# Attention and a gated feed-forward in one kernel: one more staging slot, another order of the opening, two buffers for values and earlier reads of the probabilities

## Chip, cores and metric

The kernel runs on one core of one Trainium2 chip. The metric is device time in microseconds (us) of one execution, lower is better; it stands as the median of three runs. TensorE is PE in the profile (PEld is its weight load), VectorE is DVE, ScalarE is ACT, GpSimd is POOL, SyncE is SP.

## What is computed

Attention with 4 batches, 8 heads, 768 positions and a head size of 64 comes first. A key is kept if it is one of the first 8 (global) or at most 95 positions back (local); every head adds a bias that falls with the distance. Then come 3072 tokens of a feed-forward network with a product as its gate.

```python
scores = scale * np.matmul(q, k.transpose(0, 1, 3, 2))
...
bias = -slopes[:, None, None] * dist[None, :, :]
scores = scores + bias[None, :, :, :]
scores = np.where(keep, scores, -1000000000.0)
scores = scores - np.max(scores, axis=-1, keepdims=True)
a = np.exp(scores)
a = a / (np.sum(a, axis=-1, keepdims=True) + 1e-09)
return np.matmul(a, v).astype(np.float32)
...
a = x @ w1
b = x @ w2
h = a * b @ w3
return (h @ w_out).astype(np.float32)
```

w1 and w2 are 512 x 1024, w3 is 1024 x 1024, w_out is 1024 x 512. The weights reach the kernel as 64-bit words, and the kernel turns them into 32-bit floats itself.

## The kernel before

The tokens are cut into 12 chunks of 256. A step takes two of the four head pairs of a chunk, so there are 24 steps, numbered from 0. Numbers that matter are kept as a high and a low part (names ending in h and l), so that one product is three matmuls. Since h @ w_out follows with nothing between, w3 and w_out are first multiplied together: `fold` (L197) sums eight matmuls for one of eight row blocks f, ACT copies the sum to wh (L199), and `low` (L205, on DVE) writes the low part wl.

**What a step does.** `visit` (L650) issues the scores of step s on PE (L488) and the product of earlier probabilities with their values (L597) in two halves; ahead of the second half stands a small ACT copy into the sums (L662). `rows` takes the row extreme on DVE (L504) and the exponential on ACT (L505); `invert` and `softmax` scale the rows (L509 and L510 on DVE, L521 on ACT, L523 on DVE). In steps 0 to 2 the probabilities are turned by PE (L532, L534) and copied by ACT into the tile early (L536, L538). From step 3 on DVE transposes blocks of 32 (L558), SP writes them to DRAM (L560, tile d), and `back` reads them again in another order (L568, tile ph): four reads, two issued by SP and two by ACT. `take` (L57, L58, L635, L640) moves the results of a visit to xh and xl or xr.

Visit s of the opening, up to visit 3, uses the probabilities of step s - 1; from step 5 on visit s uses those of s - 2. Queries with keys (qr, L466) and values (vr, L473) have one buffer each. vr of step s - 1 is loaded during step s, after the visit.

**The feed-forward.** `run` is a generator, and `slices(k)` runs k of its pieces between the parts of a step. A piece is twelve matmuls of a first product (L220 to L222, into m), or some of the last (L241 to L243). After the first of two products ACT copies it (L228) into ring_a; after the second DVE multiplies the two (L230); gh and gl are the parts of that (L232, or L57 and L58).

**The opening.** `first_steps` runs the words of `ORDER`, which sets the order of DVE, SP and PE by hand (ACT is ordered by the scheduler there). `c` and `C` convert one piece of a weight (`begin`: L151, `merge`: L164, the high part on ACT L169, the low part on DVE L181 or, for `C`, on ACT L172 and a DMA of POOL); `fXY` and `r` are folds, `lX` is L205 of block X, `vX` a visit, `aX` its rows, `sX` its scaling (and the loads behind that), `tXY` a turn, `kX` a take, `pX` or `p` a piece of the feed-forward, `q` the low parts that are due. `ORDER3` does the same for step 3. Each weight lands in a numbered slot `raw[n]`, by the list `plan`; a load is issued when every piece that was in its slot is converted.

**The later steps** are a plain loop; PE, ACT, SP and POOL run in the order in which the code is written, DVE in that of the scheduler. From step 7 on every second step adds one row block of the first weights for the end (`mix`, POOL, L859 and L862, into tiles tq and tl); `round_off` (ACT L867 into th, POOL L869) and `keep` (L873, L874, the stores of th and tl to DRAM, tile tw) follow in the next steps. From step 23 on (about 393 us) the last tokens run as products by Strassen's scheme, which read tw back.

Of the kernel before, what the change touches and what calls it, by code (L numbers as in the profile page):

```python
# [10 lines left out]
F32 = mybir.dt.float32  # L11
F32R = mybir.dt.float32r
BF16 = mybir.dt.bfloat16
I32 = mybir.dt.int32
AF = mybir.ActivationFunctionType
ALU = mybir.AluOpType
PSUM = bass.MemoryType.PSUM

B, H, S, D = 4, 8, 768, 64
DM, DF, DO = 512, 1024, 512  # L20
P = 128
NP = H // 2
NQ = 2
# [3 lines left out]
NCC = DM // P  # L27
NFC = DF // P
# [18 lines left out]
c x c C c C f00 z c C f20 f10 f30 C f31 c C m f21 c c f32 c f11 f01 f13 f12 f23 f22 f33 f03 f34 c c f04 x c v0 f15 f14 f05 f24 f25 f02 f16 f07 f27 f26 a0 f17 f36 f35 f06 C s0 r f37 r r t01 r r l2 r c r r t00 r l1 l0 c c v1 r l3 r c r a1 r c l4 r r s1 r r k1 r r t10 r r t11 r r v2 c r l5 r r r c r a2 r q c l6 r s2 k2 r r p C t20 l7 p t21 c p  # L47
# [28 lines left out]
class FeedForward:  # L76
# [3 lines left out]
    def __init__(self, ctx, tc, w1, w2, w3t, w_out, out):  # L80
        self.nc = tc.nc
# [125 lines left out]
    def run(self, c, xh, xl, row, width, last=False):  # L207
# [4 lines left out]
        for f0 in range(0, NFC, nf):  # L212
# [17 lines left out]
            nc.vector.tensor_tensor(out=a, in0=ps, in1=a, op=ALU.mult)  # L230
# [174 lines left out]
def banded(ctx, tc, ff, xp, ns, nt, nf, oki, ident, qk, vx):  # L405
# [22 lines left out]
    ff.more_room(xp)  # L428
    ff.raw[8] = early.bitcast(I32).rearrange("p i m k c -> p i (m k c)")
# [39 lines left out]
    def load_values(c, hp, tag="vr"):  # L469
        b, cb = divmod(c, NCB)  # L470
        nw = 2 * NQ if cb else 2 * NQ - 1
        vr = ld.tile([P, STEP, 2 * NQ, 2 * D], F32, tag=tag, name=f"vr_{c}_{hp}")
        nc.sync.dma_start(out=vr[:, :, :nw], in_=vx[b, cb, hp // STEP, :, :, :nw])  # L473
        return [vr[:, i] for i in range(STEP)]
# [87 lines left out]
    def back(s):  # L562
        if s not in sent:
            return
        x, d = sent.pop(s)
        for b, m0 in enumerate((1, 0, 3, 2)):
            ms = slice(m0, m0 + 5)
            (nc.sync, nc.scalar)[b // 2].dma_start(out=x[b * BK:(b + 1) * BK].rearrange("r k a u c -> r (k a) (u c)")[:, ms], in_=d[:, :, :, b].rearrange("k a r e -> r (k a) e")[:, ms])  # L568
        phs[s] = x
# [138 lines left out]
    def first_steps():  # L708
# [24 lines left out]
        for i in (0, 1, 0, 1, 0):  # L733
            clear(i)
        plan = ["nt", ("a0", 0, 1), ("o0", 0, 0), ("t0", 0, 1), ("o1", 1, 0), ("t1", 1, 1), ("o2", 2, 0), ("t2", 2, 1), ("o3", 3, 0), ("t3", 3, 1), ("o4", 4, 0), ("t4", 4, 1), ("o5", 0, 0), ("t5", 0, 1), "qr",
                ("o6_7", 1), ("t6_7", 2), ("b0", 3), ("b1", 4), ("b2", 5), ("b3", 2), ("w0", 4), ("w1", 6), ("w2", 5), ("w3", 7), ("w4", 6), ("w5", 4), ("w6", 7), ("w7", 4)]
# [117 lines left out]
    def mix(f):  # L854

        th, tl = tg.tile([P, 4, 2 * P], F32R, name="th"), tg.tile([P, 4, 2 * P], F32, name="tl")
        q = tg.tile([P, 2, NCC * P], F32, name="tq")
        for i in range(2):
            nc.gpsimd.tensor_tensor(out=q[:, i], in0=ff.wq[0][:, f, i].bitcast(F32), in1=ff.wq[1][:, f, i].bitcast(F32), op=ALU.add)  # L859
        (b11, b21), (b12, b22) = ((q[:, i, :2 * P], q[:, i, 2 * P:]) for i in range(2))  # L860
        for o, x, y in ((2, b12, b11), (0, b22, tl[:, 2]), (1, b22, b12), (3, b21, tl[:, 0])):
            nc.gpsimd.tensor_tensor(out=tl[:, o], in0=x, in1=y, op=ALU.subtract)  # L862
        mixed.append((f, th, tl))
# [13 lines left out]
    with tc.manual_schedule(engines={mybir.EngineType.PE}):  # L877
        with tc.manual_schedule(engines={mybir.EngineType.DVE, mybir.EngineType.SP}):
            first_steps()
        with tc.manual_schedule(engines={mybir.EngineType.Activation, mybir.EngineType.SP, mybir.EngineType.Pool}):  # L880
            for s in range(SWAP + 1, n):
# [3 lines left out]
                for i, p in enumerate(pairs(s)):  # L885
                    rs.append(rows(*p, ps[i]))
                    if i == 0 and uu is not None:
                        take(sv, uu)
                loads(s + 1, vals=False)
                loads(s - 1, keys=False)  # L890
                back(s - 1)
                if 0 <= s - MIX < 2 * NFC and (s - MIX) % 2:
                    round_off()
# [4 lines left out]
                if mixed:  # L898
                    keep()
                if 0 <= s - MIX < 2 * NFC and (s - MIX) % 2 == 0:  # L900
                    mix((s - MIX) // 2)
                slices(SLICES[s] - 2)
            back(n - 1)
            vrs[n - 1] = load_values(*pairs(n - 1)[0], tag="qr")
# [214 lines left out]
```

## Time and profile before

| | us |
|---|---|
| runs | 532.54, 532.24, 531.98 |
| median of the three | 532.24 |
| the profiled execution | 533.92 |
| its span, first to last instruction | 532.1 |
| PE busy in it | 519.6 |
| DVE, ACT, POOL busy | 338.6, 256.9, 71.4 |

The profiled execution is 1.68 us above the median of the runs, and 1.82 us of its time lie outside its span. TensorE ran at a mean granted clock of 0.999. PE is busy for 98% of the span, so a time that some other engine takes matters only where PE has to stop for it. Busy PE contains the overlap of matmuls that run one behind the other: what a stop costs is read from the starts of two matmuls.

### The profile page before, as it was taken

The numbers are of one execution on the slowest core, as the hardware profiler recorded it, in microseconds if no ns is written. First come the engines' busy times: TensorE is split into PE (matmuls) and PEld (weight loads), VectorE is DVE, ScalarE is ACT, GpSimd is POOL, SyncE is SP. The second block draws the span as 40 slices with busy tenths as digits, with TensorE's granted clock in tenths as the row PEclk, the third lists the DMA queues.
The fourth block names the chain that finished last, engine by engine and source line by source line (L and its number), as shares of the span: only waits on it lengthen the run. The fifth ranks groups of instructions, "written<-read, shape, count | busy, mean of one in ns | idle before, by whom it ended". The sixth has DMA issues, their size and how long they took to land.

```text
span 532.1 us, 11252 instructions
## 1 busy us (share of the span) xinstructions
PE 519.6 (98%) x4260; PEld 412.8 (78%) x4260; DVE 338.6 (64%) x906; ACT 256.9 (48%) x729; POOL 71.4 (13%) x87
## 2 busy tenths in 40 slices
PE   8899999999899999999999999999999999999996
PEld 3345469989888888888888888788888888888884
DVE  7999997976687576665767646687535433434400
ACT  0344776576566554556665554677424322222220
POOL 0000000000225050243215033422000000000000
PEclk9999999999999999999999999999999999999999
DMA  8997855377779766876857598988724322222031
GB/s 303 407 347 247 306 168 184 120 259 238 224 237 289 256 208 204 264 257 205 274 205 251 161 322 246 275 257 281 218 65 132 111 93 80 79 89 70 1 120 44
DMA packets 50653, 107.70 MB, mean 202 GB/s; under 512 B 4768, under 2 KB 28576, under 8 KB 50592
## 3 DMA queue, kind: packets, MB, share of 16 engines
q1 hardware_dynamic: 43056, 99.50, 54.9%
q10 hardware_dynamic: 7392, 6.88, 5.5%
q0 software_dynamic: 144, 0.52, 0.5%
q8 instruction: 35, 0.57, 0.5%
q14 instruction: 26, 0.21, 0.1%
HBM read 69.67 MB, written 36.70 MB: 200 GB/s over the span
## 4 chain that ended last, share of the span: by engine, by line
PE 78%; DVE 14%; DMA 4%; issue 2%; ACT 1%; SPq 1%; ACTq 0%; DVEq 0%
PE m L220 10%; PE m L221 9%; PE m L222 9%; PE a L948 8%; PE o L241 6%; PE o L242 5%; PE o L243 5%; PE v L597 5%; PE s L488 5%; PE ob L968 4%; PE oa L968 4%; PE b L948 4%; PE c L948 2%; DVE t3s L164 2%; DVE wo L164 2%
## 5 line engine op out<-in xcount | busy, mean ns | idle before, releaser
L220 PE MATMUL m<-xh,wqh 128*128 128x512 f32 (+1 forms) x320 | 113.6, 355 | 1.8 <-DVE ring_a L230 1.2
L221 PE MATMUL m<-xl,wqh 128*128 128x512 f32 (+1 forms) x320 | 111.0, 347 | 0.0
L222 PE MATMUL m<-xh,wql 128*128 128x512 f32 (+1 forms) x320 | 110.9, 347 | 0.0
L505 ACT ACTIVATE pr<-pr,mx 128x232 f32<-128x232 f32 (+1 forms) x192 | 88.2, 462 | 10.3 <-DVE mx L504 10.3
L220 PEld LDWEIGHTS m<-xh,wqh 128*128 128x128 f32 x320 | 60.4, 189 | 11.7 <-DVE ring_a L230 1.6
L222 PEld LDWEIGHTS m<-xh,wql 128*128 128x128 f32 x320 | 60.5, 189 | 7.7
L504 DVE CUSTOM_DVE_ANT_0 pr<-s,biasw 128x232 f32<-128x232 f32 x160 | 54.0, 395 | 19.2 <-PE s L488 19.2
L221 PEld LDWEIGHTS m<-xl,wqh 128*128 128x128 f32 x320 | 60.6, 189 | 7.2
L558 DVE STREAM_TRANSPOSE ph<-pr 128x512 f32<-128x512 f32 x84 | 49.1, 641 | 3.2 <-ACT pr L521 2.1
L241 PE MATMUL o<-wh,gh 128*128 128x512 f32 x128 | 50.8, 397 | 0.0
L242 PE MATMUL o<-wl,gh 128*128 128x512 f32 x128 | 49.9, 390 | 0.0
L243 PE MATMUL o<-wh,gl 128*128 128x512 f32 x128 | 49.9, 389 | 0.0
L57 ACT ACTIVATE gh<-ring_a 128x512 fp32r<-128x512 f32 x29 | 18.3, 630 | 50.8 <-DVE ring_a L230 48.0
L230 DVE TENSOR_TENSOR ring_a<-m,ring_a 128x512 f32<-128x512 f32 x32 | 21.8, 683 | 26.2 <-PE m L222 25.7
L869 POOL TENSOR_TENSOR tl<-tl,th 128x512 f32<-128x512 f32 x16 | 21.8, 1384 | 111.4 <-ACT th L867 111.4
L488 PE MATMUL s<-qr 64*64 64x168 f32 (+2 forms) x768 | 36.6, 299 | 0.0
L505 ACT ACTIVATION_READ_ACCUMULATOR pr<-pr,mx 128x1 f32 x192 | 36.2, 189 | 0.0
L597 PE MATMUL v<-ph,vr 64*64 64x64 f32 (+2 forms) x1208 | 34.1, 243 | 1.4 <-DMA ph<-d 1.4
L521 ACT ACTIVATE pr<-pr,sm 128x232 f32<-128x232 f32 (+1 forms) x84 | 33.3, 466 | 2.5 <-DVE sm L510 2.5
L597 PEld LDWEIGHTS v<-ph,vr 64*64 64x64 f32 (+1 forms) x1208 | 32.1, 133 | 2.9 <-DVE mx L504 1.6
L523 DVE TENSOR_SCALAR pr<-pr,sm 128x232 f32<-128x232 f32 (+1 forms) x84 | 30.1, 400 | 1.3
L197 PE MATMUL w<-wo,ta 128*128 128x512 f32 x64 | 29.2, 601 | 1.6 <-DVE ta L164 1.6
(154 smaller groups left out, 849.8 us busy)
## 6 DMA issues: line engine op xcount, KB each, us to landing
d<-ph SPq DMA_DIRECT2D x42, 512.0 KB, 3.4
qr<-qk SPq DMA_DIRECT2D x16, 624.0 KB, 4.5
vr<-vx SPq DMA_DIRECT2D x17, 512.0 KB, 7.0
t<-tw SPq DMA_DIRECT2D x32, 256.0 KB, 3.2
ph<-d SPq DMA_DIRECT2D x42, 160.0 KB, 7.3
ph<-d ACTq DMA_DIRECT2D x42, 160.0 KB, 6.7
out_dram<-ring_o SPq DMA_DIRECT2D x24, 256.0 KB, 2.8
raw<-w3t SPq DMA_DIRECT2D x11, 512.0 KB, 9.4
```

What stands on the lines that cost most here:

```text
L220: nc.tensor.matmul(ps[:, z], lhsT=mh, rhs=xh[:, i], start=i == 0, stop=False)
L221: nc.tensor.matmul(ps[:, z], lhsT=mh, rhs=xl[:, i], start=False, stop=False)
L222: nc.tensor.matmul(ps[:, z], lhsT=ml, rhs=xh[:, i], start=False, stop=i == NCC - 1)
L241: nc.tensor.matmul(ps, lhsT=gh[:, f, ts], rhs=self.wh[:, f], start=f == 0, stop=False)
L242: nc.tensor.matmul(ps, lhsT=gh[:, f, ts], rhs=self.wl[:, f], start=False, stop=False)
L243: nc.tensor.matmul(ps, lhsT=gl[:, f, ts], rhs=self.wh[:, f], start=False, stop=f == NFC - 1)
L488: nc.tensor.matmul(ps[u][g * HQ:(g + 1) * HQ, j, cols], lhsT=m[:, q0:q0 + HQ], rhs=m[:, j * SLOT:][:, cols], start=True, stop=True)
L504: nc.vector.tensor_tensor_reduce(out=pr[:, j, u, w0:], in0=ps[u][:, j, w0:UW], in1=bias, scale=-SCALE, scalar=3.0e38, op0=ALU.add, op1=ALU ...
L505: nc.scalar.activation(pr[:, j, u, w0:], pr[:, j, u, w0:], AF.Exp, bias=m, scale=-1.0, accum_out=sm[:, j, u:u + 1])
L558: nc.vector.transpose(x[:, k, :, u1 - 4 + u0:u1], units[:, u0:, k0:k0 + P].rearrange("p u (b c) -> p b u c", c=BK))
L597: nc.tensor.matmul(uu[i][u * D:(u + 1) * D, j * P + q:j * P + q + n], lhsT=v[r], rhs=x[:, q // step:(q + n) // step][r], start=k == 0 and ...
L948: nc.tensor.matmul(ps, lhsT=a, rhs=b, start=first and k == 0 and i == 0, stop=k == HC - 1 and i == 2, skip_group_check=True)
```

## The change

The edits, in the order of the diff:

- `ORDER`: l3 moves to right behind l0; l4 to before a1; l6 from behind the conversion of a weight to before `r q c`; s2 behind `k2` and two folds, where it stood ahead of k2; one more piece `p` between l7 and t21.
- The product L230 (L231 after the change) is marked as high priority for the scheduler of DVE.
- A staging slot 9 of 8 KB per partition (two rows of 1024 words): it shares its room with the tiles of `mix`, which now are one tile (tt) in place of th, tl and tq. Weights w4 and w7 go to slot 9 (before: 6 and 4).
- Values have two buffers; in the loop vr of step s, not of s - 1, is loaded in step s. The last values no longer use the room of qr.
- All four reads of the probabilities are issued by SP, and in the loop `back` stands ahead of the loads of qr and vr.
- `round_off` stands behind softmax and `send` of its step, `keep` in the step after that, behind the loads.

Lines after the change are higher by one to three: L505 is L507, L521 is L523, L538 is L540, L568 is L570, L662 is L664, L232 is L233, L509 and L510 are L511 and L512.

```diff
--- before.py
+++ after.py
@@ -44,7 +44,7 @@
 W = 2 * T
 TAIL = 8
 ORDER = """
-c x c C c C f00 z c C f20 f10 f30 C f31 c C m f21 c c f32 c f11 f01 f13 f12 f23 f22 f33 f03 f34 c c f04 x c v0 f15 f14 f05 f24 f25 f02 f16 f07 f27 f26 a0 f17 f36 f35 f06 C s0 r f37 r r t01 r r l2 r c r r t00 r l1 l0 c c v1 r l3 r c r a1 r c l4 r r s1 r r k1 r r t10 r r t11 r r v2 c r l5 r r r c r a2 r q c l6 r s2 k2 r r p C t20 l7 p t21 c p
+c x c C c C f00 z c C f20 f10 f30 C f31 c C m f21 c c f32 c f11 f01 f13 f12 f23 f22 f33 f03 f34 c c f04 x c v0 f15 f14 f05 f24 f25 f02 f16 f07 f27 f26 a0 f17 f36 f35 f06 C s0 r f37 r r t01 r r l2 r c r r t00 r l1 l0 l3 c c v1 r r c r l4 a1 r c r r s1 r r k1 r r t10 r r t11 r r v2 c r l5 r r r c r a2 l6 r q c r k2 r r s2 p C t20 l7 p p t21 c p
 """
 ORDER3 = "a0 p p p x S0 p a1 l p w0 p S1 w1 l p K p p l"
 SLOPES = [2.0 ** -(h + 1) for h in range(H)]
@@ -78,7 +78,7 @@
 
 
     def __init__(self, ctx, tc, w1, w2, w3t, w_out, out):
-        self.nc = tc.nc
+        self.tc, self.nc = tc, tc.nc
         self.src = (w1, w2)
         self.w3t, self.w_out, self.out = w3t, w_out, out
         self.wp = wp = ctx.enter_context(tc.tile_pool(name="wp", bufs=1))
@@ -227,7 +227,8 @@
                     a = self.slot(0).rearrange("p (n w) -> p n w", n=nf)
                     nc.scalar.activation(a, ps, AF.Copy)
                     yield
-            nc.vector.tensor_tensor(out=a, in0=ps, in1=a, op=ALU.mult)
+            with self.tc.high_priority():
+                nc.vector.tensor_tensor(out=a, in0=ps, in1=a, op=ALU.mult)
             if self.defer:
                 nc.scalar.activation(gh[:, fs], a, AF.Copy)
                 self.late.append((gl[:, fs], a, gh[:, fs]))
@@ -426,6 +427,7 @@
     biasw = bp.tile([P, H, UW], BF16, name="biasw")
 
     ff.more_room(xp)
+    ff.raw[9] = tg.tile([P, 2, 2 * PC], I32, tag="tt", name="raw_9")
     ff.raw[8] = early.bitcast(I32).rearrange("p i m k c -> p i (m k c)")
     it = early.bitcast(I32).rearrange("p i m k c -> p (i m k c)")[:, :UW]
     itg = early.bitcast(I32)[:, 1, 0, 0]
@@ -466,10 +468,10 @@
         nc.sync.dma_start(out=qr[:, :, k0:], in_=qk[b, cb, hp // STEP, :, :, k0:])
         return [qr[:, i] for i in range(STEP)]
 
-    def load_values(c, hp, tag="vr"):
+    def load_values(c, hp):
         b, cb = divmod(c, NCB)
         nw = 2 * NQ if cb else 2 * NQ - 1
-        vr = ld.tile([P, STEP, 2 * NQ, 2 * D], F32, tag=tag, name=f"vr_{c}_{hp}")
+        vr = ld.tile([P, STEP, 2 * NQ, 2 * D], F32, tag="vr", bufs=2, name=f"vr_{c}_{hp}")
         nc.sync.dma_start(out=vr[:, :, :nw], in_=vx[b, cb, hp // STEP, :, :, :nw])
         return [vr[:, i] for i in range(STEP)]
 
@@ -565,7 +567,7 @@
         x, d = sent.pop(s)
         for b, m0 in enumerate((1, 0, 3, 2)):
             ms = slice(m0, m0 + 5)
-            (nc.sync, nc.scalar)[b // 2].dma_start(out=x[b * BK:(b + 1) * BK].rearrange("r k a u c -> r (k a) (u c)")[:, ms], in_=d[:, :, :, b].rearrange("k a r e -> r (k a) e")[:, ms])
+            nc.sync.dma_start(out=x[b * BK:(b + 1) * BK].rearrange("r k a u c -> r (k a) (u c)")[:, ms], in_=d[:, :, :, b].rearrange("k a r e -> r (k a) e")[:, ms])
         phs[s] = x
 
     def views(s, i, m):
@@ -733,7 +735,7 @@
         for i in (0, 1, 0, 1, 0):
             clear(i)
         plan = ["nt", ("a0", 0, 1), ("o0", 0, 0), ("t0", 0, 1), ("o1", 1, 0), ("t1", 1, 1), ("o2", 2, 0), ("t2", 2, 1), ("o3", 3, 0), ("t3", 3, 1), ("o4", 4, 0), ("t4", 4, 1), ("o5", 0, 0), ("t5", 0, 1), "qr",
-                ("o6_7", 1), ("t6_7", 2), ("b0", 3), ("b1", 4), ("b2", 5), ("b3", 2), ("w0", 4), ("w1", 6), ("w2", 5), ("w3", 7), ("w4", 6), ("w5", 4), ("w6", 7), ("w7", 4)]
+                ("o6_7", 1), ("t6_7", 2), ("b0", 3), ("b1", 4), ("b2", 5), ("b3", 2), ("w0", 4), ("w1", 6), ("w2", 5), ("w3", 7), ("w4", 9), ("w5", 4), ("w6", 7), ("w7", 9)]
         got, held, formed = [], {}, set()
 
         def empty(*slots):
@@ -853,8 +855,9 @@
 
     def mix(f):
 
-        th, tl = tg.tile([P, 4, 2 * P], F32R, name="th"), tg.tile([P, 4, 2 * P], F32, name="tl")
-        q = tg.tile([P, 2, NCC * P], F32, name="tq")
+        tt = tg.tile([P, 2, 4, 2 * P], F32, tag="tt", name=f"tt_{f}")
+        th, tl = tt[:, 0].bitcast(F32R), tt[:, 1]
+        q = tt[:, 0].rearrange("p o c -> p (o c)").rearrange("p (n c) -> p n c", n=2)
         for i in range(2):
             nc.gpsimd.tensor_tensor(out=q[:, i], in0=ff.wq[0][:, f, i].bitcast(F32), in1=ff.wq[1][:, f, i].bitcast(F32), op=ALU.add)
         (b11, b21), (b12, b22) = ((q[:, i, :2 * P], q[:, i, 2 * P:]) for i in range(2))
@@ -886,22 +889,22 @@
                     rs.append(rows(*p, ps[i]))
                     if i == 0 and uu is not None:
                         take(sv, uu)
+                f, late = divmod(s - MIX, 2)
+                back(s - 1)
                 loads(s + 1, vals=False)
-                loads(s - 1, keys=False)
-                back(s - 1)
-                if 0 <= s - MIX < 2 * NFC and (s - MIX) % 2:
-                    round_off()
+                loads(s, keys=False)
+                if mixed and not late:
+                    keep()
                 slices(2)
                 for p, r in zip(pairs(s), rs):
                     softmax(*p, *r, nc.vector)
                 send(s, rs)
-                if mixed:
-                    keep()
-                if 0 <= s - MIX < 2 * NFC and (s - MIX) % 2 == 0:
-                    mix((s - MIX) // 2)
+                if mixed and late:
+                    round_off()
+                elif 0 <= f < NFC and not late:
+                    mix(f)
                 slices(SLICES[s] - 2)
             back(n - 1)
-            vrs[n - 1] = load_values(*pairs(n - 1)[0], tag="qr")
             x0 = xs[TAIL // 2]
             ah = {k: both(xp, t, k) for k, t in (("a11", "xh"), ("a12", "xl"))}
             for i, y in enumerate(ah.values()):
```

How the order moves, at three places. **DVE in the opening**, between the rows of step 2 (the last L504) and the rows of step 3; w_482 (w_483 after) is block 6 of the folded weight, w_568 (w_569) block 7. Before:

```order
142 L504 ISA mx_1_592 128x1
143 L181 TENSOR_TENSOR wql<-t3s,wqh 128x1024
144 L164 SCALAR_TENSOR_TENSOR t3s<-ta,t3s 128x1024
145 L151 TENSOR_SCALAR t3s<-raw_119 128x1024
146 L164 SCALAR_TENSOR_TENSOR t3s<-ta,t3s 128x1024
147 L205 TENSOR_TENSOR wl<-w_482,wh 128x512
148 L509 TENSOR_SCALAR both_580<-both_580 128x8
149 L510 RECIPROCAL both_580<-both_580 128x8
150 L58 TENSOR_TENSOR xl_383<-v_2_510,xh_382 128x2x256
151 L164 SCALAR_TENSOR_TENSOR t3s<-raw_119,t3s 128x1024
```

and after:

```order
142 L506 ISA mx_1_593 128x1
143 L205 TENSOR_TENSOR wl<-w_483,wh 128x512
144 L181 TENSOR_TENSOR wql<-t3s,wqh 128x1024
145 L164 SCALAR_TENSOR_TENSOR t3s<-raw_121,t3s 128x1024
146 L151 TENSOR_SCALAR t3s<-raw_119 128x1024
147 L164 SCALAR_TENSOR_TENSOR t3s<-raw_121,t3s 128x1024
148 L58 TENSOR_TENSOR xl_385<-v_2_511,xh_384 128x2x256
149 L511 TENSOR_SCALAR both_581<-both_581 128x8
150 L512 RECIPROCAL both_581<-both_581 128x8
151 L164 SCALAR_TENSOR_TENSOR t3s<-raw_119,t3s 128x1024
```

The low part of block 6 goes from the end of this stretch to its start, and the reciprocals change places with L58.

**ACT around visit 3** (v_0_704 before, v_0_720 after). Before:

```order
66 L228 ACTIVATE ring_a<-m_0_0_630 128x512
67 L538 ACTIVATE early<-t_1_674 128x1024
68 L662 ACTIVATE v_0_704<-ident 128x2
69 L169 ACTIVATE wqh<-t3s 128x1024
70 L172 ACTIVATE wql<-t3s 128x1024
71 L505 ACTIVATE pr_2_760,sm_2_762<-pr_2_760,mx_2_761 128x232 x4
72 L232 ACTIVATE gh_628<-ring_a 128x512
```

and after:

```order
67 L228 ACTIVATE ring_a<-m_0_0_633 128x512
68 L540 ACTIVATE early<-t_1_688 128x1024
69 L169 ACTIVATE wqh<-t3s 128x1024
70 L172 ACTIVATE wql<-t3s 128x1024
71 L233 ACTIVATE gh_631<-ring_a 128x512
72 L664 ACTIVATE v_0_720<-ident 128x2
73 L507 ACTIVATE pr_2_776,sm_2_778<-pr_2_776,mx_2_777 128x232 x4
```

The copy that opens the second half of the visit stood first of these and now stands behind the conversion of w6 and the first gh.

**SP from the opening into the loop**; the loads of w7 (raw_119 before, raw_121 after), of qr and vr for visit 3, and a step of the loop. Before:

```order
32 L466 DMA qr_2_619<-qk 128x1248
33 L473 DMA vr_0_621<-vx 128x1024
34 L141 DMA raw_119<-w 128x1024 x2
35 L473 DMA vr_2_756<-vx 128x1024
...
47 L252 DMA out_dram<-ring_o 128x512
48 L466 DMA qr_2_1351<-qk 128x2x520
49 L473 DMA vr_2_1353<-vx 128x1024
50 L568 DMA ph_2_1203<-d_2_1204 32x5x256 x2
```

and after:

```order
32 L141 DMA raw_121<-w 128x1024 x2
33 L468 DMA qr_2_627<-qk 128x1248
34 L475 DMA vr_0_629<-vx 128x1024
35 L475 DMA vr_2_772<-vx 128x1024
...
47 L253 DMA out_dram<-ring_o 128x512
48 L570 DMA ph_2_1204<-d_2_1205 32x5x256 x4
49 L468 DMA qr_2_1356<-qk 128x2x520
50 L475 DMA vr_0_1358<-vx 128x2x384
```

w7 goes ahead of the two loads for visit 3, and in the loop the reads go ahead of qr and vr.

## Rows read from the trace of the kernel before

**Rows 1.** The page: busy time, share of the span and instructions of each engine.
```profile
PE 519.6 (98%) x4260; PEld 412.8 (78%) x4260; DVE 338.6 (64%) x906; ACT 256.9 (48%) x729; POOL 71.4 (13%) x87
```
**Rows 2.** Waits of PE: who released it; us in total, times, longest us.
```profile
PE v L597 <- DMA ph<-d: 1.4, 1, 1.4
PE m L220 <- DVE ring_a L230: 1.2, 2, 0.7
PE t L532 <- ACT early L538: 0.7, 1, 0.7
PE m L220 <- ACT ring_a L228: 0.6, 1, 0.6
PE w L197 <- DVE wl L205: 0.5, 1, 0.5
```
**Rows 3.** Timeline of PE, visits 6 and 7: start us, us busy, what.
```profile
127.12 0.73 PE L488 MATMUL s<-qr 64*64 64x64 f32 x16
...
129.65 0.39 PE L220 MATMUL m<-xh,wqh 128*128 128x256 f32 x1
...
138.47 0.73 PE L488 MATMUL s<-qr 64*64 64x64 f32 x16
...
142.69 0.39 PE L220 MATMUL m<-xh,wqh 128*128 128x256 f32 x1
```
**Rows 4.** Chain of waits before visit 7: start us, us, what.
```profile
129.78 1.83 SPq L473
...
132.14 8.29 DMA ph<-d
```
**Rows 5.** The page, DMA issues: count, KB each, us to landing.
```profile
ph<-d SPq DMA_DIRECT2D x42, 160.0 KB, 7.3
ph<-d ACTq DMA_DIRECT2D x42, 160.0 KB, 6.7
```
**Rows 6.** Timeline of ACT, step 20.
```profile
334.17 1.05 ACT L867 ACTIVATE th<-tl 128x1024 fp32r<-128x1024 f32 x1
```
**Rows 7.** Timeline of DVE in the opening; in brackets the idle time before.
```profile
71.22 1.22 DVE L181 TENSOR_TENSOR wql<-t3s,wqh 128x1024 fp32r<-128x1024 f32 x1
...
76.14 0.65 DVE L58 TENSOR_TENSOR xl<-v,xh 128x512 fp32r<-128x512 f32 x1
...
80.84 0.68 DVE L205 TENSOR_TENSOR wl<-w,wh 128x512 fp32r<-128x512 f32 x1
...
86.55 0.69 DVE L151 TENSOR_SCALAR t3s<-raw 128x1024 int32<-128x1024 int32 x1 [2.76 <-DMA raw<-w]
```
**Rows 8.** Timeline of ACT in the opening.
```profile
72.57 0.58 ACT L199 ACTIVATE wh<-w 128x512 fp32r<-128x512 f32 x1
...
76.32 3.15 ACT L521 ACTIVATE pr<-pr,both 128x232 f32<-128x232 f32 x8
...
84.50 0.17 ACT L662 ACTIVATE v<-ident 128x2 f32<-128x2 f32 x1 [1.08 <-PE v L597]
...
89.38 1.04 ACT L172 ACTIVATE wql<-t3s 128x1024 fp32r<-128x1024 f32 x1
...
92.22 0.62 ACT L232 ACTIVATE gh<-ring_a 128x512 fp32r<-128x512 f32 x1
```
**Rows 9.** Timeline of PE up to visit 3, and its second half.
```profile
80.91 0.33 PE L532 MATMUL t<-ident,pr 128*128 128x128 f32 x1 [0.74 <-ACT early L538]
...
81.76 0.37 PE L220 MATMUL m<-xh,wqh 128*128 128x256 f32 x1
...
83.15 0.28 PE L222 MATMUL m<-xh,wql 128*128 128x256 f32 x1
...
83.47 0.90 PE L597 MATMUL v<-early,vr 64*64 64x128 f32 x32
...
85.33 0.86 PE L597 MATMUL v<-early,vr 64*64 64x128 f32 x32
```
**Rows 10.** Timeline of SP: the loads for visit 3, then w7.
```profile
70.63 0.43 SPq L473 DMA_DIRECT2D vr<-vx  x1
...
80.95 1.17 SPq L141 DMA_DIRECT2D raw<-w  x2
```

## The prediction

> **What bounds the kernel now.** I read the page first: PE is busy for 519.6 of 532.1 us [rows 1], so every other engine matters only where PE stops for it. Then the waits of PE name the stops that the change can reach [rows 2]: one of 1.4 us for the reads of probabilities, two of 1.2 together for the DVE product, 0.7 for a turn's copy, 0.6 for an ACT eviction, 0.5 for a low part of a folded weight. Third, the timelines tell where each lies and what it costs. The first five stops lie at 48, 81, 97, 140 and 149 us, the eviction at 335; between them, up to about 393 us, PE runs through. So the change can win some 4 us at most before that, and can lose wherever it makes a new stop.
>
> A stop costs more than its idle time. Visit 6 takes 129.65 - 127.12 = 2.53 us, visit 7 takes 142.69 - 138.47 = 4.22 [rows 3]: 1.69 us for 1.4 of idle. I therefore count each stop as its idle time and 0.2 for the restart.
>
> **Reads first (step 7).** The chain before visit 7 [rows 4] shows why the reads are late: SP stands for 1.83 us on the load of vr, which may not overwrite values that visit 6 still uses, the reads come behind it, and then take 8.29 us. In the change nothing in front of a step's reads waits for the visit, so they start at least the 1.83 us earlier, and are no longer behind the bytes of qr and vr. PE needs them 1.4 us sooner than they come. That is covered even if they take no less time: **-1.7 us**. qr of the next step is now behind four reads on SP, two more issues of about 0.4 us each; it has a step of 11 us (127.12 to 138.47) to land in. vr of step s is needed two steps later. Both cost nothing.
>
> All four reads now come from SP. The rows show reads issued by SP landing after 7.3 us and those of ACT after 6.7 [rows 5], so neither issuer had a visible lead. No row shows four from one issuer: the bounds are 0 (the same landing) and twice 7 us (SP's would queue up). I take 0, as it is nearest to the two rows; the other is a rival. Here the Trainium skill (DMA: Bandwidth & Descriptors, "Issuing engines are not separate DMA queues") bears: DMAs from several engines run on the same 16 engines, and a second issuer saves only the time to initiate them. By that rule the term is the two extra issues on SP; by separate queues it would be the 7 us.
>
> **round_off later (step 20).** There ACT runs the 1.05 us copy of mix [rows 6] and only then the eviction that PE waits for, 0.6 idle [rows 2]. Behind softmax, the copy no longer stands ahead of that eviction: 0.6 + 0.2 = **-0.8 us**. What is next: the copy stands ahead of a later eviction of the same step, as in other steps where no stop shows. The new order lets mix of the next block start only when both stores of tt have landed. Its ACT copy comes a whole step later, so I put this at 0; bounds 0 and the same 0.8 at one step more.
>
> **Product first.** Of the two DVE stops, that at 149 us (0.5) follows a DVE instruction that was slow beside POOL's mix; the order of DVE after the change still has the scaling ahead of it. Bounds 0 and -0.7; I take 0. The other, 97 us (0.7 + 0.2), goes: one more piece of the first product runs ahead of visit 3, so the product that held PE up is long done: **-0.9 us**.
>
> **The opening.** l3 earlier removes the 0.5 stop at 48 us, but l4 now stands ahead of the rows of step 1, whose chain to visit 2 becomes later by about that much. For PE I take 0 by visit 2; bounds -0.7 and 0. The weight load that waits for the folds of that place is 0.6 earlier, and DVE and ACT with it.
>
> Then l6. Before, DVE runs from 71.22 to 83.79 without a gap (86.55 less the 2.76 idle) [rows 7]. After, l6's low part comes first in this stretch, but it needs the high part, ACT's L199, which ends at 73.05 [rows 8] and stands behind six exponentials; less 0.6, that is 72.5. DVE gets there at 70.6: a **new idle of 1.9 us** in a stretch with none to spare. The same instructions follow, so all of it is 1.9 - 0.6 = 1.3 later. xl (L58), with two reciprocals now behind it, ends near 77.7 in place of 76.7; the reciprocals come at 78.05 in place of 76.1, and ACT's eight scalings start at 78.2, not 76.32 [rows 8]. l7's low part goes from 80.84 to 82.1 [rows 7] and ends at 82.8. It frees the PSUM buffer of the next first product.
>
> PE can thus start that product at 82.85. A piece takes 83.15 - 81.76 + 0.1 = 1.5 us and the turn 81.76 - 80.91 = 0.85 [rows 9]. Two pieces with the turn between them end at 82.85 + 1.5 + 0.85 + 1.5 = 86.7: visit 3. Before it started at 83.47 [rows 9] with one piece fewer: with it 84.95. **+1.75 us.**
>
> In visit 3, the small copy that opens the second half waited on PE before, at 84.50 [rows 8]. Now it stands behind the conversion of w6 (two of 1.04) and gh (0.62) [rows 8]. DVE finishes w6 after l7 with the work that took 83.79 - 81.44 and 88.3 - 86.55 before (the gap of 2.76 left out) [rows 7]: 82.8 + 2.35 + 1.75 = 86.85. ACT needs 2.6 more: 89.4, copy done 89.6. PE is ready for it 85.33 - 83.47 = 1.86 after the start [rows 9], at 88.55: **+1.05 us**.
>
> Slot 9 removes DVE's wait of 2.76 for w7 [rows 7]. DVE's own time is no PE time, so this is worth nothing by itself; it shows in that visit 4 finds everything ready. In exchange w7 goes ahead of qr and vr for visit 3 on SP: these were issued at 70.63 and w7 at 80.95 [rows 10]; now w7 waits for w4's conversion, about 77.2, and vr follows near 78.6, 8.1 us before visit 3. I take 0 for it.
>
> **Sum.** -1.7 - 0.8 - 0.9 + 1.75 + 1.05 = -0.6 us. The profiled execution took 533.92, of which 532.1 is span; it would take 533.3. It is 1.68 above the median of the runs, so against 532.24 the forecast is **531.6**. A measurement of this kernel can tell about 0.2%, 1.06 us, from no change: the likeliest outcome is one that is hard to see, two gains nearly paid back in the opening.
>
> **Rivals.**
> A, faster: DVE's new idle is there but PE does not feel it, because the pieces of the first product stretch over it and the copy in visit 3 comes in time. Then only the gains are left: -0.9 - 1.7 - 0.8 = -3.4, 528.8. For it: PE has 12 more matmuls to fill the time. Against: those matmuls need the very buffer that l7 frees.
> B, slower: vr for visit 3 comes late. Place: SP at 77 to 79 us. If the loads land one after the other, w7 takes 86.55 - 80.95 = 5.6 us from 77.2, and vr, at the longest 8.29 of [rows 4], lands at 91.1 instead of before 86.7. Visit 3 is 4.4 later, the 1.05 is hidden in that: +3.35, 534.9. It decides from a landing over 8.1 us after the issue on. Against: reads behind 1.1 MB needed 8.29 at most.
> C, slower: SP's four reads queue up, 14 us. With a step of 11 us that makes a stop in most of 18 steps, several us at least: over 537.
> D: the terms are right in kind but cancel, or the reads still come late: 532.2.
>
> **How the numbers follow.** Forecast 0.5, own range 530.6 to 532.8 (0.7 of bounds for l3, the product and round_off, and half a us for the replay); A 0.25; B 0.12; C 0.03; D 0.10. The range 528.8 to 533.4 takes in the forecast, D, most of A and the mild part of B. Faster by over 0.2% means below 531.18: A and a third of the forecast, 0.25 + 0.17 = 0.42. Slower means above 533.30: B, C and the worst of the forecast, 0.12 + 0.03 + 0.03 = 0.18. The same: 0.40.
>
> **What would show it.** Right: visit 7 takes about 2.5 us, the eviction stop of step 20 and that at 97 us are gone; a DVE idle near 2 us before l6's low part, released by ACT's L199; visit 3 starting near 86.7 with a stop of 1 us before its second half, released by the ACT copy. Wrong: no such DVE idle, or one with visit 3 before 85.5 (then A); visit 3 released by a load (B); PE stops on reads in many steps (C); ACT's mix copy waiting on POOL.

## The result and the profile after

| | before | after |
|---|---|---|
| median of the runs, us | 532.24 | 535.11 |
| lowest and highest of five runs | 531.98, 532.54 | 534.56, 535.96 |
| the profiled execution | 533.92 | 535.11 |
| its span | 532.1 | 533.3 |
| PE busy in it | 519.6 | 522.2 |

The changed kernel is slower: the ratio of the runs is 1.0052, with a 95% interval of 1.0040 to 1.0064, some 2.8 us. The forecast was 531.6 with a range up to 533.4. The two profiled executions differ by 1.2 us only. The execution profiled before stood 1.68 above its median, the one after is at its median. So the difference of the two traces is not that of the medians, and the first thing to explain is what the earlier trace holds that most executions do not.

The waits of PE after the change, the ones before 10 us among them (PE, line, released by; us in total, times, longest us):

```profile
PE w L197 <- DVE ta L164: 1.6, 3, 1.1
PE s L733 <- DVE wo L727: 1.5, 1, 1.5
PE m L221 <- DVE xl L58: 0.7, 1, 0.7
PE m L220 <- DVE ring_a L231: 0.7, 2, 0.5
PE m L220 <- ACT ring_a L228: 0.5, 1, 0.5
PE t L534 <- ACT pr L523: 0.4, 1, 0.4
PE t L534 <- ACT early L540: 0.4, 1, 0.4
PE v L599 <- ACT v L664: 0.2, 1, 0.2
```

Against [rows 2], the wait for the reads is gone and that for an eviction is about as long, though at another place (below). Three are new in the opening: for xl, for the scaled rows of a turn, and for the small copy ahead of visit 3's second half.

DVE in the opening shows the forecast idle time, 1.88 us where 1.9 was forecast (before the change there was none in this stretch, [rows 7]):

```profile
72.81 0.69 DVE L205 TENSOR_TENSOR wl<-w,wh 128x512 fp32r<-128x512 f32 x1 [1.88 <-ACT wh L199]
```

PE then stops twice between 77 and 80 us, reaches visit 3 at 87.62 and waits for the copy:

```profile
78.16 0.39 PE L221 MATMUL m<-xl,wqh 128*128 128x256 f32 x1 [0.71 <-DVE xl L58]
...
79.92 0.33 PE L534 MATMUL t<-ident,pr 128*128 128x128 f32 x1 [0.42 <-ACT pr L523]
...
87.62 0.90 PE L599 MATMUL v<-early,vr 64*64 64x128 f32 x32
...
89.91 0.90 PE L599 MATMUL v<-early,vr 40*64 40x128 f32 x32 [0.24 <-ACT v L664]
```

ACT, in the order of the second excerpt on the change, explains the last of these (to be read with [rows 8]): the copy runs only when conversion and gh are through.

```profile
87.27 1.06 ACT L169 ACTIVATE wqh<-t3s 128x1024 fp32r<-128x1024 f32 x1
88.24 1.04 ACT L172 ACTIVATE wql<-t3s 128x1024 fp32r<-128x1024 f32 x1
89.19 0.61 ACT L233 ACTIVATE gh<-ring_a 128x512 fp32r<-128x512 f32 x1
89.70 0.15 ACT L664 ACTIVATE v<-ident 128x2 f32<-128x2 f32 x1
```

Busy time by stretch (the second number is its length, then PE, PEld, DVE, ACT, POOL, the granted TensorE clock, the DMA share and GB/s), after the change:

```profile
79.00:80.00 1.00, 0.54 (x4) 0.28 (x4) 1.00 (x2) 1.00 (x4) 0.00 (x0) 1.00 0.76 279
80.00:84.00 4.00, 4.00 (x20) 3.64 (x21) 3.97 (x5) 4.00 (x9) 0.00 (x0) 0.57 1.02 416
84.00:88.00 4.00, 4.00 (x48) 3.87 (x50) 3.41 (x5) 2.27 (x3) 0.00 (x0) 1.00 0.45 182
```

After the two stops the clock falls from its full level to half; over 80 to 84 us it is 0.57 in the mean, and two neighbouring matmuls of the product start 0.21 us apart there, 0.12 after it. Visit 3 starts 0.9 later than forecast, and its second half, which waits for ACT, at 89.91, forecast 89.6.

What the clock costs here can be read from e2 (below), the same opening in front of the old loop. Its trace runs some 0.2 us later (l6's low part at 73.02, against 72.81 here) and keeps the full clock:

```profile
80.00:84.00 4.00, 3.24 (x23) 2.68 (x24) 3.96 (x5) 4.00 (x9) 0.00 (x0) 1.00 1.02 419
...
90.12 0.90 PE L598 MATMUL v<-early,vr 40*64 40x128 f32 x32 [0.75 <-ACT v L663]
```

Visit 3 starts there at 87.33, so half of the 0.9 is the clock. But its second half starts at 90.12, which less these 0.21 is 89.91 again, and visit 4 at 105.52 against 105.32. So the clock costs nothing here: the copy on ACT hides it. The five runs agree, as the two with a mean granted clock of 0.999 and 1.000 took 535.39 and 535.96, the three with 0.995 and 0.996 took 534.56 to 535.11. The opening as a whole comes out as forecast (1.75 + 1.05 - 0.9 = 1.9): visit 4 starts at 105.32, before at 103.23, and the earliest visit at 25.72 in place of 25.52, so 1.9 us are the opening's own.

Visit 7 shows the other half:

```profile
140.56 0.73 PE L490 MATMUL s<-qr 64*64 64x64 f32 x16
...
143.09 0.39 PE L220 MATMUL m<-xh,wqh 128*128 128x256 f32 x1
```

It takes 2.53 us in place of 4.22 [rows 3]. So in the two traces the mechanism of the reads is as forecast; the experiments ask whether this gain is one of the kernel or of one execution.

### The profile page after: what moved, and what is told of

The parts are those of the page before. It is cut to its first block, busy times and chain, and to the rows that moved or that the text cites. A ratio compares the mean times of both kernels' runs of the same rounds, so it can differ in the third digit from the quotient of the medians.

```text
span 533.3 us, 11169 instructions
## 1 busy us (share of the span) xinstructions
PE 522.2 (98%) x4260; PEld 413.9 (78%) x4260; DVE 335.7 (63%) x906; ACT 256.6 (48%) x729; POOL 70.8 (13%) x87
## 4 chain that ended last, share of the span: by engine, by line
PE 73%; DVE 14%; DMA 5%; ACT 4%; issue 2%; SPq 1%; DVEq 0%; ACTq 0%
PE m L220 9%; PE m L221 9%; PE m L222 9%; PE a L951 8%; PE o L242 5%; PE o L243 5%; PE o L244 5%; PE s L490 4%; PE v L599 4%; PE ob L971 4%; PE oa L971 4%; PE b L951 4%; DMA d<-ph 3%; DVE t3s L164 2%; PE c L951 2%
## 5 line engine op out<-in xcount | busy, mean ns | idle before, releaser
L507 ACT ACTIVATE pr<-pr,mx 128x232 f32<-128x232 f32 (+1 forms) x192 | 88.2, 461 | 15.9 <-DVE mx L506 15.9
L231 DVE TENSOR_TENSOR ring_a<-m,ring_a 128x512 f32<-128x512 f32 x32 | 21.7, 677 | 25.0 <-PE m L222 24.8
L507 ACT ACTIVATION_READ_ACCUMULATOR pr<-pr,mx 128x1 f32 x192 | 36.1, 188 | 0.0
L862 POOL TENSOR_TENSOR tt<-wqh,wql 128x512 f32<-128x512 f32 x16 | 21.2, 1344 | 98.8 <-DMA tw<-tt 98.8
L523 ACT ACTIVATE pr<-pr,sm 128x232 f32<-128x232 f32 (+1 forms) x84 | 33.0, 464 | 1.5 <-DVE sm L512 1.5
L58 DVE TENSOR_TENSOR gl<-ring_a,gh 128x512 fp32r<-128x512 f32 x29 | 24.9, 860 | 13.1 <-ACT gh L57 12.8
```

Of the source, the lines that this page charges most:

```text
L507: nc.scalar.activation(pr[:, j, u, w0:], pr[:, j, u, w0:], AF.Exp, bias=m, scale=-1.0, accum_out=sm[:, j, u:u + 1])
```

## Experiments

Each was timed beside new runs of the kernel before; ratios are against those. In the medians of these batches the kernel before took 532.2 to 532.6 us, its single runs 531.5 to 534.1.

**The loop alone, the opening alone.** First edit: `ORDER` and the slots of w4 and w7 as before, everything else changed. Second edit: the loop, `load_values`, the issuers of the reads and the product's priority as before, the rest changed.

```diff
# e1: ORDER as before, and in plan
- ... ("w4", 9), ("w5", 4), ("w6", 7), ("w7", 9)]
+ ... ("w4", 6), ("w5", 4), ("w6", 7), ("w7", 4)]
# e2: in the loop, among other lines
+                loads(s + 1, vals=False)
+                loads(s - 1, keys=False)
+                back(s - 1)
+                if 0 <= s - MIX < 2 * NFC and (s - MIX) % 2:
+                    round_off()
```

> The changed kernel with the old order of the opening and the old slots for w4 and w7; the loop as changed. Theory 1 (the loss lies in the opening: stops of PE at 75 to 80 us, and then about 3 us at half the clock; the loop by itself gains, as its stop of 1.7 at visit 7 and of 0.9 at 335 are gone and new ones of about 1.6 in all are smaller): faster than before by about 0.5 to 1 us, 531.2 to 531.8, no clock below 1.0 between 75 and 90 us. Rival (the loss lies in the loop, its new small stops at 163, 180, 191, 352 and 364 us): about as slow as the whole change, 534 to 535.

> The changed kernel with the loop of the kernel before (reads behind the loads, two by ACT, values loaded a step later from one buffer, round_off and keep at their old places, no priority for the product); the order of the opening, slot 9 and the joint tile as changed. Theory 1: slower than before by about 2.1 us, 534.3, with the clock at half between 80 and 84 us, and the old stop at visit 7. Rival (loss in the loop): 532 to 532.5.

Measured: the loop alone 532.7 us, ratio 1.0008 (0.9998 to 1.0018); the opening alone 534.47, ratio 1.0043 (1.0030 to 1.0056), with the clock at its full level from 80 to 84 us. So 2.3 of the 2.8 us are the opening, and they do not need the clock to fall: that part of theory 1 is wrong. The loop brings no gain (between 0.1 us faster and 1.0 slower), where I had counted 2.5 us. Both parts of the sum are thus to be explained.

Where the loop pays shows in the starts of visits 20, 21 and 23, before and then after the whole change:

```profile
328.38 0.80 PE L488 MATMUL s<-qr 64*64 64x168 f32 x16
...
341.44 0.80 PE L488 MATMUL s<-qr 64*64 64x168 f32 x16
...
366.10 0.80 PE L488 MATMUL s<-qr 64*64 64x168 f32 x16
```

```profile
329.79 0.80 PE L490 MATMUL s<-qr 64*64 64x168 f32 x16
...
341.97 0.80 PE L490 MATMUL s<-qr 64*64 64x168 f32 x16
...
367.67 0.80 PE L490 MATMUL s<-qr 64*64 64x168 f32 x16
```

Step 20 becomes 0.88 us shorter (13.06 to 12.18) and steps 21 and 22 together 1.04 longer (24.66 to 25.70). The trace of e1 has the same, 0.87 against 1.01. In the whole change steps 8 and 10 are 0.25 and 0.74 longer as well; in e1 they are 0.16 and 0.05. The profiled execution of e1 is the fastest of its eleven, 1.1 us below their median, so what the median loses beyond this stays open.

**l6, and l6 with s2, back.** In the changed kernel:

```diff
# e3, in ORDER
- ... a2 l6 r q c r k2 r r s2 p C ...
+ ... a2 r q c l6 r k2 r r s2 p C ...
# e4, in ORDER
- ... a2 l6 r q c r k2 r r s2 p C ...
+ ... a2 r q c l6 r s2 k2 r r p C ...
```

> The changed kernel with l6 alone back at its old place, behind the conversion of a weight. Theory 1a (l6's wait of 1.9 us for ACT delays DVE, that makes PE's stops, these pull the clock down): DVE without that idle, PE's stops at 77 and 79 us smaller or gone, clock at 1.0 from 80 to 84; 2 us or more faster than the whole change, 532.5 to 533. Rival 1b (s2's move and the extra piece make the stops whatever l6 does): no more than 0.7 us faster, 534.4 or more, clock still at half there.

> The changed kernel with l6 and s2 both at their old places; l3, l4, slot 9 and the extra piece stay. Theory 1a: hardly different from putting l6 back alone, within 0.5 us of it. Rival 1b: this one is 1.5 us or more faster than l6 back alone, since the scaling and the loads for visit 3 come earlier again.

Measured: 533.3 us, ratio 1.0024 (1.0014 to 1.0034), and 533.2, ratio 1.0020 (1.0011 to 1.0029). l6's place alone costs 1.8 us of the whole (535.11 less 533.3; by the two ratios 1.5), s2's nothing that these runs can tell. With l6 back DVE has no gap at this place:

```profile
74.00 1.21 DVE L164 SCALAR_TENSOR_TENSOR t3s<-raw,t3s 128x1024 int32<-128x1024 int32 x1
75.13 0.68 DVE L205 TENSOR_TENSOR wl<-w,wh 128x512 fp32r<-128x512 f32 x1
```

About 0.7 us over the loop alone is left. In both traces visit 3 takes 3.6 us, with 0.8 of waiting for the small copy.

**The kernel before again, for its trace.** No edit.

> The kernel before, unchanged, for a second trace. Its profiled execution stood 1.7 us above the median of its runs, and the stop at visit 7 cost 1.69. Theory 2 (that stop belongs to the one execution that was profiled, not to the median): here the span is near 530.4, and visit 7 takes between 2.5 and 3.4 us, not 4.2. Rival (the stop is in every run, and the loop change gives its gain back elsewhere): visit 7 takes 4.0 us or more at any span.

Measured: 533.13 us with a span of 531.3, not near 530.4. Visit 7 starts at 138.79 and ends where the next product starts:

```profile
141.67 0.39 PE L220 MATMUL m<-xh,wqh 128*128 128x256 f32 x1
```

That is 2.88 us, not 4.22: 0.36 over visit 6's 2.52. In the traces of five other kernels with the old order of the reads (e2, e8, e9, e10, e12) the visit took 3.33, 2.52, 3.23, 3.07 and 2.52. So the stop is 0 to 0.8 us in these six, 0.4 in the mean, and 1.69 in the execution that I read. The read that was issued last took 8.29 us to land in that execution and 6.4 to 7.7 in the six. (In e2 and e9 the rows put the wait down to DVE, but the last read landed 0.14 before PE went on, much as in the trace before with 0.13.) The stop does not explain all of that execution's distance from the median: this second one has 1.33 less of it and is only 0.8 shorter, as its first visit starts 0.5 later and its end is 0.4 longer.

**The reads ahead of the loads, alone.** In the kernel before:

```diff
+                back(s - 1)
                 loads(s + 1, vals=False)
                 loads(s - 1, keys=False)
-                back(s - 1)
```

> The kernel before with one edit: the reads of the probabilities stand ahead of the loads of qr and vr in the loop (still two by SP and two by ACT). Theory 2: visit 7 takes 2.5 us in the trace, yet the time is that of before within 0.5 us, 531.8 to 532.5, since most executions had little of this stop. Rival (the stop is in every run): faster by about 1.5 us, 530.5 to 531.

Measured: 534.86 us, ratio 1.0039 (1.0026 to 1.0051): slower by 2 us, which neither theory had expected. Visit 7 takes 2.52, but visit 9 is late: of PE's waits the longest is

```profile
PE s L488 <- DMA qr<-qk: 1.9, 1, 1.9
```

SP, in this kernel, ahead of visit 9:

```profile
155.84 0.80 SPq L568 DMA_DIRECT2D ph<-d  x2
156.74 0.38 SPq L466 DMA_DIRECT2D qr<-qk  x1
```

and in the kernel before (whose PE is some 2 us later at this place):

```profile
154.26 0.33 SPq L466 DMA_DIRECT2D qr<-qk  x1
154.76 0.55 SPq L473 DMA_DIRECT2D vr<-vx  x1
156.48 0.80 SPq L568 DMA_DIRECT2D ph<-d  x2
```

The reads stand on SP until the blocks are in DRAM (the second write landed at 155.79 here, the reads were issued at 155.84). Behind the loads this wait cost nothing; ahead of them qr of the next step waits as well, and landed at 162.78, where PE wanted it at 161.0. After PE's wait the clock fell as well, in the same trace:

```profile
162.00:163.00 1.00, 0.09 (x4) 0.12 (x8) 0.00 (x0) 0.00 (x0) 0.96 (x1) 1.00 1.08 391
163.00:166.00 3.00, 3.00 (x52) 2.56 (x56) 1.37 (x8) 0.39 (x2) 0.00 (x0) 0.50 1.03 419
```

and visit 9 took 4.19 us, 2.41 in the trace before. So in this trace the clock nearly doubles the price of the wait: the step before visit 9 is 1.94 longer than before, the step after it 1.75. In the whole change the same place shows 0.18 of idle released by qr, and the step before it is 0.25 longer, in the loop alone 0.16. Why so little is left there (all four reads on SP, two buffers for values) was not tried.

**No extra piece.** The changed kernel with l6, s2 and the pieces as before; l3, l4 and slot 9 stay.

```diff
- ... a2 l6 r q c r k2 r r s2 p C t20 l7 p p t21 c p
+ ... a2 r q c l6 r s2 k2 r r p C t20 l7 p t21 c p
```

> The changed kernel with l6, s2 and the number of pieces p as before; of the opening only l3, l4 and slot 9 stay changed. Theory 3 (what the opening still costs with l6 back, 0.6 to 1 us, is the second half of visit 3, which stands behind w6's conversion and gh on ACT because the extra piece makes gh come first): visit 3 takes 2.65 in place of 3.63 us, a stop of 0.4 to 0.9 comes back near 97 us, and the time falls by 0.4 to 0.8, to 532.4 to 532.9. Rival (it is slot 9, with w7 ahead of the loads for visit 3, or l4 ahead of the rows of step 1): the same as with l6 and s2 back, 533.1 or more.

Measured: 535.91 us, ratio 1.0060 (1.0044 to 1.0076): slower than the whole change. Theory 3 falls, and so does its rival, which had expected the time of e4. The extra piece is no cost, it covers one: visit 3 now takes 4.78 us, 1.91 of it waiting for the small copy, though gh is not ahead of that copy any more. Conversion of w6 alone is. After this wait the clock fell:

```profile
89.00:92.40 3.40, 3.40 (x18) 3.40 (x18) 1.29 (x2) 1.08 (x4) 0.00 (x0) 0.50 0.82 154
```

Of the six runs the two with a mean granted clock of 0.998 took 534.16 and 534.36, the four with 0.995 to 0.997 took 535.54 to 536.53. So most of the 2.7 us over e4 may be the clock and not the wait itself; about 1 us is left without it.

**Slot 9 alone.** The kernel before with w4 and w7 in slot 9 (and the joint tile that makes the room), and the same with the last conversion issued behind visit 3.

```diff
# e9, to the kernel before
- ... ("w4", 6), ("w5", 4), ("w6", 7), ("w7", 4)]
+ ... ("w4", 9), ("w5", 4), ("w6", 7), ("w7", 9)]
# e10, to e9
- ... p C t20 l7 p t21 c p
+ ... p C t20 l7 p t21 p
-ORDER3 = "a0 p p p ...
+ORDER3 = "c a0 p p p ...
```

> The kernel before with slot 9 alone (w4 and w7 go there, the tiles of mix are joined to make the room); order of the opening and loop as before. Theory 5 (the slot itself is the cost of the opening that l6 does not explain: DVE no longer waits for w7, so ACT's conversion of w6 is ordered ahead of the small copy that opens the second half of visit 3, and PE waits for it): visit 3 takes 4.5 us or more in place of 2.65, released by that copy; 2 us or more slower than before, 534.3 to 536. Rival (l3 and l4 made the loss of the kernel without the extra piece): within 0.7 us of before.

> As with slot 9 alone, with one more edit: the last conversion before visit 3 is issued behind the visit, which puts the small copy ahead of w6's conversion on ACT and leaves DVE's order nearly as it was. Theory 5: visit 3 takes about 2.7 us, no drop of the clock there; within 0.7 us of before, 1.5 us or more faster than slot 9 alone. Rival (the loads for visit 3, now behind w7 on SP, are what visit 3 waits for): as slow as slot 9 alone.

Measured: slot 9 alone 534.79 us, ratio 1.0048 (1.0035 to 1.0061). With the copy ahead of the conversion 531.64, ratio 0.9986 (0.9978 to 0.9995). 3 us lie between two kernels that differ in the place of one copy of 0.15 us on ACT (and in the order of two neighbouring conversions on DVE). A part of the 3 us may again be the clock, though the trace of e9 has it full here: the three runs with 0.998 or 0.999 took 533.73 to 534.41, the three with 0.996 or 0.997 took 535.16 to 535.56. ACT and PE with slot 9 alone:

```profile
85.84 1.06 ACT L169 ACTIVATE wqh<-t3s 128x1024 fp32r<-128x1024 f32 x1 [2.27 <-DVE t3s L164]
86.80 1.04 ACT L172 ACTIVATE wql<-t3s 128x1024 fp32r<-128x1024 f32 x1
87.75 0.15 ACT L663 ACTIVATE v<-ident 128x2 f32<-128x2 f32 x1
```

```profile
87.96 0.90 PE L598 MATMUL v<-early,vr 40*64 40x128 f32 x32 [2.19 <-ACT v L663]
```

and with the copy first:

```profile
84.98 0.17 ACT L663 ACTIVATE v<-ident 128x2 f32<-128x2 f32 x1 [1.29 <-PE v L598]
86.46 1.06 ACT L169 ACTIVATE wqh<-t3s 128x1024 fp32r<-128x1024 f32 x1 [1.30 <-DVE t3s L164]
87.42 1.04 ACT L172 ACTIVATE wql<-t3s 128x1024 fp32r<-128x1024 f32 x1
```

```profile
85.80 0.88 PE L598 MATMUL v<-early,vr 64*64 64x128 f32 x32
```

ACT stands idle for 2.27 us ahead of a conversion that waits for DVE, with the copy behind it; with the copy first it ran 1.0 us after visit 3 had started. The slot then gives what it can: PE has no stop near 97 us, with 0.7 of idle before [rows 2]. PE waits 0.26 there for vr ahead of visit 3, now behind w7 on SP (0.41 in e7, nothing in the whole change): that is all that was left of rival B.

**round_off's place.** In the kernel before, late in step 20 alone; in the loop alone (e1), early again in all steps.

```diff
# e8
-                if 0 <= s - MIX < 2 * NFC and (s - MIX) % 2:
+                if 0 <= s - MIX < 2 * NFC and (s - MIX) % 2 and s != 20:
                     round_off()
...
                 send(s, rs)
+                if s == 20:
+                    round_off()
# e11, to e1
+                if mixed and late:
+                    round_off()
                 slices(2)
...
-                if mixed and late:
-                    round_off()
-                elif 0 <= f < NFC and not late:
+                if 0 <= f < NFC and not late:
```

> The kernel before with one edit: in step 20 alone round_off stands behind softmax and send. Theory 4 (the late place is right in this step, where it stood ahead of the eviction that PE waits for, and wrong in others, where it now stands ahead of a later one): the stop of 0.7 at 335 us goes and no other comes; 0.5 to 0.8 us faster than before, 531.4 to 531.7. Rival (the late copy meets the next eviction in step 20 as well): the same time as before within 0.3 us.

> The loop change alone (old opening) with round_off back ahead of the slices. Theory 4 (the late place moves the stop of step 20 to steps 10, 21 and 22 at no gain): the stops near 350 and 361 us go, the one of 0.7 near 334 comes back; the time is that of the loop change alone within 0.5 us. Rival (the late place is a gain in itself): 0.7 us or more slower than the loop change alone, 533.3 or more.

Measured: late in step 20 alone 531.27 us, ratio 0.9979 (0.9971 to 0.9988). The stop at 335 us is gone and no other came; the ratio makes it 0.6 to 1.5 us, where I had priced 0.8. Early in the changed loop: 534.41, ratio 1.0048 (1.0036 to 1.0061), 1.7 slower than the changed loop, so the rival is right there. The stop near 334 is back, as expected, but that near 361 did not go, it grew to 1.0 us, and one of 1.0 came at 186. The trace shows how the latter comes about:

```profile
178.56 2.81 POOL L862 TENSOR_TENSOR tt<-wqh,wql 128x512 f32<-128x512 f32 x2 [18.28 <-DMA tw<-tt]
```

```profile
184.47 1.06 ACT L870 ACTIVATE tt<-tt 128x1024 fp32r<-128x1024 f32 x1 [1.24 <-POOL tt L865]
```

With one joint tile the whole of mix waits for the stores of the block before (before, its first two additions had a tile of their own), POOL ends later, and an early copy makes ACT wait for it, with the eviction behind. So with the joint tile and the late stores the early place costs more than the late one. The late place has its own price, which the whole change pays in step 22:

```profile
363.15 1.05 ACT L870 ACTIVATE tt<-tt 128x1024 fp32r<-128x1024 f32 x1
364.10 0.58 ACT L228 ACTIVATE ring_a<-m 128x512 f32<-128x512 f32 x1
```

```profile
364.72 0.50 PE L220 MATMUL m<-xh,wqh 128*128 128x512 f32 x1 [0.47 <-ACT ring_a L228]
```

It is the picture of [rows 6] two steps later: the same copy ahead of the same kind of eviction.

**The two gains together** (e10 with the edit of e8).

> The kernel before with the two edits that gained by themselves: slot 9 with the last conversion behind visit 3, and round_off behind softmax in step 20 alone. If the two places are independent, the gains add: 1.2 and 0.7 us, 530.3 to 530.8, with no stop near 97 and 335 us. Rival (one of the two gains is paid back at another place, as in the whole change): 531.3 or more.

Measured: 531.75 us, ratio 0.9978 (0.9969 to 0.9987) against a kernel before of 532.6 in this batch. Faster than both kernels of the case, as the rival had it; by the ratio 0.7 to 1.7 us, so the sum of the two gains by their ratios, 1.9, is missed, though the intervals of the three overlap. The stops near 97 and 335 us are gone, and at 359 us PE waits 1.3 for an eviction:

```profile
356.30 0.81 ACTq L569 DMA_DIRECT2D ph<-d  x2
357.15 1.06 ACT L869 ACTIVATE tt<-tt 128x1024 fp32r<-128x1024 f32 x1 [1.46 <-DMA vr<-vx]
```

The row names vr, but the two reads that ACT issues stand directly ahead, and they were issued right after the second write of the blocks had landed (356.12). ACT waits at its own DMA, with copy and eviction behind. That the wait comes in most executions was not tried; the single runs lie between 530.3 and 532.2.

## Why the prediction was wrong

The forecast was -0.6 us, measured are +2.8. By its steps:

- **The sum against the median.** "It is 1.68 above the median of the runs, so against 532.24 the forecast is 531.6" is the step that failed most. The mechanism of the reads was right, the size was that of one execution. The stop of 1.69 at visit 7 was most of what set that execution apart from its median, and I took it off the median all the same. All six other traces with the old order have 0.8 or less, two of them 0 (shown); a fair term was their mean, -0.4. That alone puts the forecast near 533.
- **"qr of the next step is now behind four reads on SP ... nothing"** failed. I had looked at the step's length and not at what the reads wait for: a write into DRAM that lands only shortly before. Alone, the edit lost 2 us by it (shown). In the whole change, with SP as the only issuer and two buffers, 0.2 to 0.3 us of it shows in the step.
- **round_off, -0.8**, with the later place of the copy put at 0: right in step 20 (e8), but "bounds 0 and the same 0.8 at one step more" should have been the term itself. Steps 21 and 22 take 1.0 us more, step 22 by the same kind of stop, so nothing is left of this gain. In the trace of the whole change step 8 (that of qr above) and step 10 lose another 1.0 us. In step 10 a part of it is a stop of 0.22 at 191 us, where the product stands behind transposes on DVE; the rest has no cause shown, and the step lost 0 to 0.88 in the traces of e1, e3, e4 and e7. By this one trace the account nearly closes: the forecast with -0.4 at visit 7 is 532.9, the two losses of 1.0 make it 534.9, measured are 535.1.
- **Product first, -0.9**: the stop at 97 us went, as forecast, but the reason given is not needed. e10, with neither the extra piece nor the priority, has no such stop either, so slot 9 is enough for it.
- **The opening, +1.75 and +1.05**: right in place and in sum, with the -0.9 the 1.9 us up to visit 4. DVE idle 1.88 (1.9), second half of visit 3 at 89.91 (89.6). The division was less good: visit 3 came 0.9 later than forecast (0.4 in e2, without the fall of the clock), and the stop before its second half was 0.24 (0.75 in e2) in place of 1.05. That fall was not in the sum, and the copy on ACT hid all of it, which was luck. l3 and l4 cancelled, as forecast: the stop at 48 us went and one of 0.41 came at 63. The opening alone cost 2.3 us in the medians.
- **Slot 9, "I take 0 for it"** was mis-sized in its parts: alone it costs 2.5 us. I had put the +1.05 of visit 3 down to gh and a late w6; slot 9 by itself, without l6's delay, puts that conversion ahead of a copy that PE needs, and this order is what costs (e9 against e10, shown). Why the scheduler orders it so, the earlier w7 being the likely reason, is argued. In the whole change l6's delay and the extra piece move visit 3 back so far that little of the wait is seen. The prediction had read this order off the schedule and so had the cost in its +1.05, under another cause: the sum was right though its parts weren't.

Of the rivals, A did not come. Nor did B in the changed kernel, whose measured time it happened to name (534.9): no visit 3 there waits for a load, and in the variants 0.41 us at most (e7). C did not come: the page of the changed kernel has all 84 reads by SP with a median of 3.6 us to landing, against 7.3 and 6.7 [rows 5].

```profile
ph<-d SPq DMA_DIRECT2D x84, 160.0 KB, 3.6
```

The Trainium skill (DMA: Bandwidth & Descriptors, "Issuing engines are not separate DMA queues") says that DMAs started by several engines run on the same 16 engines, and that several issuers save only the time to initiate them. The row is in line with that. It is no test of the issuer alone, as the reads now also stand ahead of the loads; with that order and still two issuers (e6) they landed after 4.1 us (SP) and 6.1 (ACT).

## To carry to other kernels

Before a stop of one execution enters a sum, look how far that execution is from the median, and read a second trace: here a wait for a DMA was 1.69 us in one and 0 to 0.8 in six others. When an instruction is moved ahead on a queue, ask what it waits for itself: here everything behind it inherited that wait. A resource that lets work start earlier may make a scheduler put that work ahead of a tiny instruction that the bottleneck needs: compare the order on every engine, and pin the tiny one first.

## What was not expected of the hardware

The clock of TensorE did not follow the length of a stop. In the changed kernel two idle times of 0.71 and 0.42 us between 77 and 80 us were followed by about half the clock, 1.2 in place of 2.4 GHz, in 80 to 84 us; in e2, the same opening, idle times of 0.70 and 0.42 at the same places were followed by the full clock. In e6 1.88 of idle was followed by 0.50 from 163 to 166, in e7 1.91 by 0.50 from 89 to 92.4. With slot 9 alone PE was idle 2.19 in one piece and the granted clock over 84 to 90 us stayed at 1.00, as it did at visit 7 before [rows 3] with 1.4. Which of them it will be was not settled; a new stop has a second price that may or may not come: some 1.75 us in the trace of e6, and nothing in the changed kernel, where PE had to wait for ACT anyway.
